# Retention with two mixture-of-experts layers: where the low halves of the second weight are made in the first slots

## The chip, the cores and the metric

The kernel runs on one core of a Trainium2 chip. The core has five engines with instruction queues of their own: TensorE (matrix products, called PE in the profile), VectorE (DVE), ScalarE (ACT), GpSimd (POOL) and SyncE (SP, which here issues transfers). The metric is the device time of one execution in microseconds (us), taken as the median over runs.

## The reference

The reference computes retention over 4 batches of 768 positions with 8 heads of 64 features, which gives 3072 tokens of 512 features, and passes these through two mixture-of-experts layers. Each layer sends every token to one of 8 experts, and an expert is two products with a ReLU in between. The second layer has one more gate on the output. Cut to what matters:

```python
def _moe_ref(x, modality_id, w_gate, modality_bias, w1, w2):
    logits = x @ w_gate + modality_bias[modality_id]
    e_idx = np.argmax(logits, axis=1)
    ...  # gate_w: softmax weight of the chosen expert
    for e in range(E):
        mask = e_idx == e
        h = np.maximum(x[mask] @ w1[e], 0.0)
        out[mask] = gate_w[mask, None] * (h @ w2[e])
    return out

def reference(**kwargs):
    attn_out = _attn_ref(**attn_kwargs)
    x = attn_out.transpose(0, 2, 1, 3).reshape(B * S, H * D)
    x = _moe_ref(x=x, **moe_kwargs)
    return _moe2_ref(x=x, **moe2_kwargs)
```

## The kernel before, in words

All products of the experts are done in pieces. A float32 operand is split into a high half (a copy rounded to the type fp32r, made by ScalarE) and a low half (what the rounding left, made by a subtraction), and one product becomes three: high by high, high by low, low by high. So each weight tile that is loaded (`raw1`, `raw2`) is turned into `w1h`, `w1l` and `w2h`, `w2l`. `split2` does this for the second weight: for each of four blocks of features it has ScalarE write `w2h` (L510) and an engine out of the list `los` write `w2l` (L511). A block of the second weight is a tile of 128 partitions by 1024 elements.

After retention, tokens are written to places in DRAM sorted by expert (`x1d` for the first layer, `x2d` for the second) with scatters that GpSimd issues (L469). A layer then runs over *slots* of 256 such rows, at least 12 and at most 19. A slot works like this:

- The rows are fetched (`fetch_rows`, L528 and L533), turned (L540) and split into `xh` and `xl` (L545, L547).
- The first product `mm1` (L891) runs over eight groups of 128 hidden features, 12 matmuls each, into four accumulators `hT`; after every second group `relu` has ScalarE write the high half `hh` (L882) and VectorE the low half `hl` (L883) of one of four blocks of hidden features.
- The second product `mm2` (L909) runs in eight steps of six matmuls: four steps for the first 128 rows, then four for the others. Step j uses blocks j of `hh`, `hl`, `w2h` and `w2l`; the second matmul of a step is the first that reads `w2l`.
- VectorE weighs the result (L915 or L917) and it is scattered, into `x2d` or into the output.

The routing of the tokens that a slot of layer 1 has made goes on inside the next slot, and the routing of the last tokens of the stage before goes on inside a layer's first slot. It is a chain of some 60 small VectorE steps. Logits go over `misc` (L588, or L945 to L954 in layer 2), the choice ends in `r_oh` (L207, L210), TensorE ranks the tokens (L215, L217), and from L221 on VectorE turns ranks into places, then into the table `r_meta` of the slots (to L359 the row positions, to L412 the experts). The two scatters of the last tokens follow the places, and the fetch of the next slot's rows follows these scatters.

Order is written out by hand: each engine runs its queue in the order of the code, and waits on semaphores for what the other engines produce. In `Slot.run`, `at(f)` runs the routing steps that are due at group f, then come `mm1(f)`, after odd f the `relu`, and in a layer's first slot (`first` is true) the splits of the second weight that are due at f. Later slots split the second weight only when the expert changes, in one piece and all on VectorE. The lines that the change and the prediction's steps touch are L1019 (the table of splits), L510 and L511, L882 and L883, the routing lines from L183 to L412, L469, L528, and the two products.

Of the kernel before, what the change touches and what calls it, by code (L numbers as in the profile page):

```python
# [416 lines left out]
def retention_moe_moe_kernel(ctx: ExitStack, tc: tile.TileContext, q, k, v, mod, mb, wg, wg2, w1, w2, cst_d, out):  # L417
    nc = tc.nc
# [89 lines left out]
    def split2(los=(nc.vector, nc.vector, nc.vector, nc.vector), ks=range(KF // 2)):  # L508
        for i in ks:
            nc.scalar.activation(w2h[i], raw2[i], AF.Copy)  # L510
            los[i].tensor_tensor(w2l[i], raw2[i], w2h[i], op=ALU.subtract)  # L511
# [91 lines left out]
    with ExitStack() as actx:  # L603
# [126 lines left out]
        for i in range(n):  # L730
# [37 lines left out]
            if i == 0:  # L768
# [3 lines left out]
                tr(1, "qT", "sq", halves=True)  # L772
                scale(2)
            run(*[f() for f in late.get(i, [])])
            for t in written.get(i, []):
                scatter1(t)
# [12 lines left out]
    with ExitStack() as mctx:  # L789
# [28 lines left out]
        class Slot:  # L818
# [153 lines left out]
            def steps(self, steps):  # L972
                by = {}
                for j, fs in list(steps):
                    by.setdefault(j, []).extend(fs)

                def at(j):
                    for f in by.get(j, []):
                        r = f()
                        if hasattr(r, "__next__"):  # L980
                            run(r)
                return at
# [22 lines left out]
            def run(self, steps=(), nxt=()):  # L1005

                at, first = self.steps(steps), self.first
                self.ids()
                if not first:
                    self.split2()  # L1010
                for f in range(KF):
                    at(f)
                    if f == 5:
                        self.prepare()
                    self.mm1(f)
                    if f % 2:
                        self.relu(f // 2)
                    if first:
                        split2([nc.gpsimd] * 2 + [nc.vector] * 2, ({0: (2, 0, 1), 1: (3,)}, {1: (2, 0), 2: (1, 3)})[self.li - 1].get(f, ()))  # L1019
                for j in range(8):  # L1020
                    at(8 + j)
                    if first and j == 5:
                        self.regs()
                        self.load(raw1, w1)
                        self.load(raw2, w2)
                    if j == (6 if first else 0):
                        self.split1(0)
                    if j == (7 if first else 2):
                        self.coming(nxt, Slot.xpose)
                        self.coming(nxt, Slot.xsplit)  # L1030
                        self.split1(1)
                    self.mm2(j // 4, range(2 * (j % 4), 2 * (j % 4) + 2))
                    if j % 4 == 3:
                        self.done(j // 4)
                at(16)
# [88 lines left out]
        def first2(pend):  # L1124
            g, steps = pend.route(FIRST_AT, banks=hT[2:])
            run(rp2.order())
            first(2, steps[:5], g, FIRST_AT[4], pend.scatter)
# [79 lines left out]
```

## Time and profile before

| | |
|---|---|
| median of three runs | 854.3 us (853.04 to 856.71) |
| the profiled execution | 853.39 us, of which the span from first to last instruction is 851.5 us |
| TensorE busy (matmuls) | 799.0 us, 94% of the span, mean granted clock 0.983 |
| VectorE busy | 430.3 us, 51% |
| ScalarE busy | 276.2 us, 32% |
| GpSimd busy | 202.1 us, 24% |

The first slot of layer 1 lies from about 153 to 184 us of the span, that of layer 2 from about 500 to 530 us. In a timeline row the first number is the start in us from the span's start, the second the duration in us, then come engine, line, operation, what is written and read with its shape, and how many instructions the row merges; in square brackets stands how long the engine was idle before, and what released it. In a row of stretches, the granted clock is a share of TensorE's full 2.4 GHz.

### The profile page before, as it was taken

The page shows a single profiled execution, that of the slowest core. Times are in us where ns is not written, and L with a number is a line of the kernel's source. Part 1 is how long each engine was busy: PE and PEld are TensorE (multiplying, and loading weights), DVE is VectorE, ACT ScalarE, POOL GpSimd, SP SyncE. Part 2 cuts the span into 40 slices and gives each one's busy share as a digit, 9 for nine tenths or more (in the row PEclk, how much of TensorE's full clock was granted, in tenths as well). Part 3 has the DMA queues.
Part 4 walks back from the last instruction along what each step waited for, and adds up shares of the span by engine and source line. Part 5 has one row for each costly group of instructions (what it writes and reads, how often), then busy time and mean ns, then how long its engine had stood idle before and what let it go on. Part 6 is the DMA issues. An engine that isn't in the chain of part 4 may idle for free. (4 is left out here: it accounts for less than half of the span.)

```text
span 851.5 us, 18413 instructions
## 1 busy us (share of the span) xinstructions
PE 799.0 (94%) x5987; PEld 696.2 (82%) x5987; DVE 430.3 (51%) x1110; ACT 276.2 (32%) x476; POOL 202.1 (24%) x291
## 2 busy tenths in 40 slices
PE   8999998799999998999999787999999999999992
PEld 7888877788889977888899576997889888888871
DVE  4554556744444338334454676144555673545921
ACT  3444445312122124121222451113252551514610
POOL 3455456712221011222210032011211112020210
PEclk9999999899999999999999999999999999999997
DMA  9987799272111015311222523412726385252610
GB/s 163 236 224 185 177 240 305 99 253 72 40 40 51 15 53 162 116 53 51 58 71 52 177 76 121 157 40 54 251 65 209 100 285 172 94 173 70 207 40 16
DMA packets 149688, 106.98 MB, mean 126 GB/s; under 512 B 94845, under 2 KB 125693, under 8 KB 149504
## 3 DMA queue, kind: packets, MB, share of 16 engines
q1 hardware_dynamic: 141664, 85.37, 37.2%
q0 software_dynamic: 6400, 18.98, 6.0%
q8 instruction: 73, 1.20, 0.6%
q14 instruction: 111, 0.91, 0.4%
q10 hardware_dynamic: 1440, 0.53, 0.3%
HBM read 167.64 MB, written 25.83 MB: 227 GB/s over the span
## 5 line engine op out<-in xcount | busy, mean ns | idle before, releaser
L891 PE MATMUL hT<-xh,w1h 128*128 128x256 f32 x768 | 222.4, 290 | 4.7 <-issue 2.9
L891 PE MATMUL hT<-xl,w1h 128*128 128x256 f32 x768 | 216.7, 282 | 1.4 <-DVE xl L547 1.4
L891 PE MATMUL hT<-xh,w1l 128*128 128x256 f32 x768 | 216.5, 282 | 0.0
L909 PE MATMUL po<-w2h,hh 128*128 128x512 f32 x432 | 172.6, 400 | 0.3
L909 PE MATMUL po<-w2l,hh 128*128 128x512 f32 x432 | 171.2, 396 | 0.0
L891 PEld LDWEIGHTS hT<-xh,w1h 128*128 128x128 f32 x768 | 146.4, 191 | 12.4 <-issue 11.0
L891 PEld LDWEIGHTS hT<-xl,w1h 128*128 128x128 f32 x768 | 146.6, 191 | 2.9 <-DVE xl L547 2.2
L891 PEld LDWEIGHTS hT<-xh,w1l 128*128 128x128 f32 x768 | 146.4, 191 | 0.0
L909 PE MATMUL po<-w2h,hl 128*128 128x512 f32 x432 | 136.3, 396 | 0.5 <-DVE hl L904 0.5
L883 DVE SCALAR_TENSOR_TENSOR hl<-hT,hh 128x512 fp32r<-128x512 f32 x96 | 65.5, 689 | 136.3 <-ACT hh L882 105.8
L882 ACT ACTIVATE hh<-hT 128x512 fp32r<-128x512 f32 x96 | 57.0, 596 | 201.7 <-PE hT L891 191.9
L909 PEld LDWEIGHTS po<-w2h,hl 128*128 128x128 f32 x432 | 81.1, 188 | 21.8 <-DVE hl L904 2.0
L909 PEld LDWEIGHTS po<-w2h,hh 128*128 128x128 f32 x432 | 81.6, 189 | 19.6 <-ACT hh L903 1.6
L909 PEld LDWEIGHTS po<-w2l,hh 128*128 128x128 f32 x432 | 81.6, 189 | 18.0
L469 POOL DMA_INDIRECT x2d<-ob,r_idx x28 | 29.6, 1059 | 261.0 <-DVE ob L260 174.5
L919 POOL DMA_INDIRECT out_dram<-ob,to x28 | 30.2, 1079 | 217.4 <-DVE ob L917 139.8
L545 ACT ACTIVATE xh<-xTb 128x512 fp32r<-128x512 f32 x58 | 33.5, 624 | 88.5 <-DVE xTb L540 79.7
L511 DVE TENSOR_TENSOR w2l<-raw,w2h 128x1024 fp32r<-128x1024 f32 x40 | 47.3, 1234 | 13.7 <-DMA xqb<-x1d 6.2
L506 DVE TENSOR_TENSOR w1l<-raw,w1h 128x512 fp32r<-128x512 f32 x80 | 49.8, 683 | 2.5 <-ACT w1h L505 2.5
L547 DVE TENSOR_TENSOR xl<-xTb,xh 128x512 fp32r<-128x512 f32 x58 | 37.6, 690 | 22.3 <-ACT xh L545 22.3
L505 ACT ACTIVATE w1h<-raw 128x512 fp32r<-128x512 f32 (+1 forms) x84 | 47.7, 640 | 0.0
L915 DVE TENSOR_SCALAR ob<-po,xmb 128x512 f32<-128x512 f32 x24 | 18.0, 750 | 54.5 <-PE po L909 54.5
(205 smaller groups left out, 997.9 us busy)
## 6 DMA issues: line engine op xcount, KB each, us to landing
raw<-in_w_dram SPq DMA_DIRECT2D x248, 512.0 KB
xqb<-x2d SPq DMA_DIRECT2D x124, 64.0 KB
xqb<-x1d SPq DMA_DIRECT2D x108, 64.0 KB
nq<-in_q_dram SPq DMA_DIRECT2D x24, 256.0 KB
nk<-in_k_dram SPq DMA_DIRECT2D x24, 256.0 KB
nv<-in_v_dram SPq DMA_DIRECT2D x24, 256.0 KB
x1d<-zrow SPq DMA_DIRECT2D x4, 516.0 KB
x2d<-zrow SPq DMA_DIRECT2D x4, 516.0 KB
```

The lines of the kernel that those rows point to most:

```text
L469: return nc.gpsimd.indirect_dma_start(out=dst, out_offset=bass.IndirectOffsetOnAxis(ap=rp.idx[:, t:t + 1], axis=0), in_=row, in_offset=Non ...
L505: nc.scalar.activation(w1h[i][:, cols], raw1[i][:, cols], AF.Copy)
L506: los[i].tensor_tensor(w1l[i][:, cols], raw1[i][:, cols], w1h[i][:, cols], op=ALU.subtract)
L511: los[i].tensor_tensor(w2l[i], raw2[i], w2h[i], op=ALU.subtract)
L545: nc.scalar.activation(hi[:, k:k + 2, :], xT[:, k:k + 2, :], AF.Copy)
L547: nc.vector.tensor_tensor(lo[:, k:k + 2, :], xT[:, k:k + 2, :], hi[:, k:k + 2, :], op=ALU.subtract)
L882: nc.scalar.activation(hh[b], hT[b], AF.Relu)
L883: nc.vector.scalar_tensor_tensor(hl[b], in0=hT[b], scalar=0.0, in1=hh[b], op0=ALU.max, op1=ALU.subtract)
L891: nc.tensor.matmul(to, lhsT=a[k][:, fs], rhs=b[:, k, :], start=(k == 0 and m == 0), stop=(k == KD - 1 and m == 2))
L909: nc.tensor.matmul(po[h], lhsT=x[b][:, o:o + P], rhs=w[f // 2][:, f % 2, :], start=(f == 0 and i == 0), stop=(f == KF - 1 and x is hl))
L915: nc.vector.tensor_scalar(perm(o[:, :DM]), plain(po[h]), gate, None, op0=ALU.mult)
L919: nc.gpsimd.indirect_dma_start(out=out, out_offset=bass.IndirectOffsetOnAxis(ap=to[:, t:t + 1], axis=0), in_=o[:, :DM], in_offset=None, bo ...
```

## The change

In the first slot of each layer the four low halves of the second weight were divided: blocks 0 and 1 on GpSimd, blocks 2 and 3 on VectorE, and they were done early, after groups 0 and 1 in layer 1 and after groups 1 and 2 in layer 2. Now all four are on VectorE, in the order of the blocks: in layer 1 after groups 0, 3, 5 and 7, in layer 2 after groups 1, 2, 5 and 7. The high halves, made by ScalarE in the same loop, move along. The programs of TensorE and SyncE are the same.

```diff
                     if first:
-                        split2([nc.gpsimd] * 2 + [nc.vector] * 2, ({0: (2, 0, 1), 1: (3,)}, {1: (2, 0), 2: (1, 3)})[self.li - 1].get(f, ()))
+                        split2([nc.vector] * 4, ({0: (0,), 3: (1,), 5: (2,), 7: (3,)}, {1: (0,), 2: (1,), 5: (2,), 7: (3,)})[self.li - 1].get(f, ()))
```

GpSimd's queue in layer 1's first slot, as a difference (`w2l_104` and `w2l_105` are the low halves of blocks 0 and 1; layer 2 loses the same two rows):

```order
 L854 TENSOR_SCALAR valid<-xmf,cst 128x1
 L856 COPY ob_2157<-xmf 128x2
-L511 TENSOR_TENSOR w2l_104<-raw_88,w2h_100 128x1024
-L511 TENSOR_TENSOR w2l_105<-raw_89,w2h_101 128x1024
 L469 DMA x1d<-yn_127,r_idx 26624x516 x2
 L810 TENSOR_LOAD r_meta
```

The scatters L469 now follow the small steps directly.

VectorE's queue in layer 1's first slot, from the first low half to the first step after the rank product. `hl_2147` and `hl_2148` are the low halves of hidden blocks 0 and 1. Before:

```order
L511 TENSOR_TENSOR w2l_106<-raw_90,w2h_102 128x1024
L583 COPY yl_125<-xT 128x128
L883 SCALAR_TENSOR_TENSOR hl_2147<-hT_116,hh_2143 128x512
L511 TENSOR_TENSOR w2l_107<-raw_91,w2h_103 128x1024
L588 COPY r_lg<-misc 128x8
...
L190 TENSOR_TENSOR rdz_626<-r_lg,rmx_623 128x16
L201 SCALAR_TENSOR_TENSOR rq_634<-rdz_626,cst 128x16
L205 TENSOR_REDUCE rm_0_637<-rq_634 128x2
L207 TENSOR_TENSOR r_oh<-rq_634,rm_0_637 128x16
L883 SCALAR_TENSOR_TENSOR hl_2148<-hT_117,hh_2144 128x512
L221 TENSOR_TENSOR rR_691<-misc,r_base 128x24
```

And now:

```order
L511 TENSOR_TENSOR w2l_104<-raw_88,w2h_100 128x1024
L583 COPY yl_125<-xT 128x128
L883 SCALAR_TENSOR_TENSOR hl_2147<-hT_116,hh_2143 128x512
L588 COPY r_lg<-misc 128x8
...
L190 TENSOR_TENSOR rdz_626<-r_lg,rmx_623 128x16
L201 SCALAR_TENSOR_TENSOR rq_634<-rdz_626,cst 128x16
L205 TENSOR_REDUCE rm_0_637<-rq_634 128x2
L207 TENSOR_TENSOR r_oh<-rq_634,rm_0_637 128x16
L883 SCALAR_TENSOR_TENSOR hl_2148<-hT_117,hh_2144 128x512
L511 TENSOR_TENSOR w2l_105<-raw_89,w2h_101 128x1024
L221 TENSOR_TENSOR rR_691<-misc,r_base 128x24
```

The second low half on this engine moved from ahead of the logits (L588) to behind `hl` of block 1, just ahead of L221. In the same way the one of block 2 (`w2l_106`) now stands behind `hl` of block 2 inside the chain of the places, between L345 and L347. The last one stands at the end of the routing. VectorE there, before:

```order
L409 CAST snx_2374<-r_meta 128x1
L411 SCALAR_TENSOR_TENSOR r_more<-r_last,snx_2374 128x1
L412 CAST r_sel<-r_more 128x1
L883 SCALAR_TENSOR_TENSOR hl_2150<-hT_119,hh_2146 128x512
L915 TENSOR_SCALAR ob_2157<-po_120,xmf 128x4x4x32
```

And now:

```order
L411 SCALAR_TENSOR_TENSOR r_more<-r_last,snx_2372 128x1
L412 CAST r_sel<-r_more 128x1
L883 SCALAR_TENSOR_TENSOR hl_2150<-hT_119,hh_2146 128x512
L511 TENSOR_TENSOR w2l_107<-raw_91,w2h_103 128x1024
L915 TENSOR_SCALAR ob_2157<-po_120,xmf 128x4x4x32
```

The low half of block 3 has become the last thing on VectorE before the result is weighed. In layer 2 the low halves of blocks 0 and 1 keep the two places that those of blocks 2 and 3 had (behind `hl` of block 0, and behind the copy L947), the one of block 2 stands behind `hl` of block 2 and ahead of L221, and the one of block 3 behind `hl` of block 3, between L359 and L369.

## Rows read from the trace of the kernel before

**Rows 1.** TensorE's waits: line, releaser: us in total, times, longest us

```profile
PE misc L215 <- DVE r_oh L207: 6.0, 2, 4.0
PE misc L952 <- DVE lT L947: 1.9, 1, 1.9
```

**Rows 2.** Timeline of layer 1's first slot: TensorE, GpSimd and VectorE

```profile
158.44 0.37 PE L891 MATMUL hT<-xh,w1h 128*128 128x256 f32 x1
...
161.50 4.67 POOL L511 TENSOR_TENSOR w2l<-raw,w2h 128x1024 fp32r<-128x1024 f32 x2
...
161.63 4.57 DVE L190 TENSOR_TENSOR rdz<-r_lg,rmx 128x16 f32<-128x16 f32 x1
...
166.87 0.17 PE L215 MATMUL misc<-r_oh,cb 128*128 128x16 bf16 x1 [3.98 <-DVE r_oh L207]
...
167.57 0.17 DVE L221 TENSOR_TENSOR rR<-misc,r_base 128x24 f32<-128x24 f32 x1
...
170.38 0.69 DVE L883 SCALAR_TENSOR_TENSOR hl<-hT,hh 128x512 fp32r<-128x512 f32 x1 [0.47 <-ACT hh L882]
...
172.81 0.39 PE L909 MATMUL po<-w2h,hh 128*128 128x512 f32 x1
...
174.24 0.68 DVE L883 SCALAR_TENSOR_TENSOR hl<-hT,hh 128x512 fp32r<-128x512 f32 x1
...
184.01 0.28 PE L891 MATMUL hT<-xh,w1h 128*128 128x256 f32 x1
```

**Rows 3.** Stretches: us; busy PE, PEld, DVE, ACT, POOL; clock; DMA share; GB/s

```profile
150.00:151.00 1.00, 1.00 (x8) 0.92 (x6) 0.97 (x5) 0.71 (x2) 0.75 (x1) 0.52 0.76 279
167.00:173.00 6.00, 6.00 (x40) 6.00 (x38) 5.32 (x42) 0.60 (x1) 2.06 (x2) 0.72 0.23 88
486.00:487.00 1.00, 0.97 (x6) 0.93 (x7) 1.00 (x1) 0.00 (x0) 0.00 (x0) 1.00 0.86 223
```

**Rows 4.** Timeline of layer 1's first slot: two ScalarE steps, hh and w2h

```profile
158.25 0.59 ACT L882 ACTIVATE hh<-hT 128x512 fp32r<-128x512 f32 x1
...
158.73 1.06 ACT L510 ACTIVATE w2h<-raw 128x1024 fp32r<-128x1024 f32 x1
```

**Rows 5.** Timeline of layer 2's first slot: VectorE and TensorE

```profile
507.18 0.42 DVE L947 COPY lT<-misc 128x256 f32<-128x256 f32 x1
...
511.14 0.18 DVE L954 COPY r_lg<-misc 128x32 f32<-128x32 f32 x1
...
511.56 1.32 DVE L190 TENSOR_TENSOR rdz<-r_lg,rmx 128x16 f32<-128x16 f32 x1
...
513.83 0.17 PE L215 MATMUL misc<-r_oh,cb 128*128 128x16 bf16 x1 [2.63 <-DVE r_oh L210]
...
514.35 0.17 DVE L221 TENSOR_TENSOR rR<-misc,r_base 128x24 f32<-128x24 f32 x1
...
517.80 0.15 DVE L359 TENSOR_SCALAR r_meta<-sd 128x1 int32<-128x1 f32 x1
...
518.03 0.63 PE L909 MATMUL po<-w2h,hh 128*128 128x512 f32 x1
```

**Rows 6.** Layer 2, slots 1 and 2 begin: timeline, and TensorE's branch (duration ns)

```profile
532.61 0.57 PE L891 MATMUL hT<-xh,w1h 128*128 128x256 f32 x1 [2.92 <-issue]
...
L1136 PEldq COMPARE_BRANCH  x1: 6109/6109/6109, 525.5 to 525.5; - x1
...
553.32 1.29 DVE L547 TENSOR_TENSOR xl<-xTb,xh 128x512 fp32r<-128x512 f32 x2 [0.76 <-ACT xh L545]
...
556.62 0.28 PE L891 MATMUL hT<-xh,w1h 128*128 128x256 f32 x1
```

**Rows 7.** Timeline: a low half and a scatter beside it; layer 2's second scatter

```profile
155.16 1.23 DVE L511 TENSOR_TENSOR w2l<-raw,w2h 128x1024 fp32r<-128x1024 f32 x1 [0.96 <-ACT w2h L510]
...
155.57 1.66 POOL L469 DMA_INDIRECT x1d<-yn,r_idx  x1 [0.30 <-issue]
...
517.97 0.97 POOL L469 DMA_INDIRECT x2d<-ob,r_idx  x1 [0.30 <-issue]
```

## The prediction, written before the change was run

> **What bounds the kernel now.** I read the page first: TensorE is busy 94% of the span and every other engine about half or less, so only what makes TensorE wait, or lowers its clock, can move the time. The list of TensorE's waits comes next [rows 1]. Its largest entries are waits of the rank product (L215) for `r_oh`, a small table that VectorE makes; one entry of 6.0 us for two waits has a longest of 4.0. That longest one stands in the stretch that the diff touches, layer 1's first slot, and the timeline shows why [rows 2]: VectorE's tiny L190 (16 elements a partition) runs 4.57 us, from 161.63 to 166.20, while GpSimd runs its two low halves of the second weight (L511) from 161.50 to 166.17. The two end together. L190 leads to `r_oh`, so TensorE waits 3.98 us before 166.87. The price does not end there. Over 167 to 173 the granted clock is 0.72 [rows 3], the lower of the two levels (1.2 GHz) for about half of the stretch. The same picture stands in layer 2's first slot [rows 5]: L190 takes 1.32 us where its neighbours take about 0.17, and the rank product waits 2.63 us.
>
> **Part by part, layer 1's first slot.** *Removed: GpSimd's two passes.* With them gone I let L190 take about 0.17. In the new order VectorE has no low half between `hl` of block 0 and the logits, so `r_oh` is made from about 159.5 on and is there near 161.2. TensorE would come to the rank product at 166.87 - 3.98 = 162.89. The wait goes whole: 3.98 us. The clock: from 158.44 to 162.89 TensorE ran 36 matmuls (three groups) in 4.45 us; from the rank product at 166.87 to the second product at 172.81 it ran 36 again and took 5.94 [rows 2]. So the slow stretch cost 1.49 us, and it goes with the wait. The second product starts at 172.81 - 5.47 = 167.3.
>
> *Added: two more low halves on VectorE, 1.23 us each [rows 7], in new places.* What is late next is the last one. Follow VectorE: block 1's sums are full after two of the three groups, at 158.44 + 24/36 x 4.45 = 161.4. ScalarE makes `hh` (0.59) and then the high half (1.06) [rows 4], which is ready at 163.1; the low half of block 1 ends at 164.4. Only then comes L221, the first step of the ranking. Before, L221 began at 167.57 and `hl` of block 3 at 174.24 [rows 2]; take off the 0.47 that VectorE waited in between (its row at 170.38) and the chain is 6.20 long. Now the low half of block 2 lies inside it: 164.4 + 6.2 + 1.2 = 171.8. Then `hl` (about 0.6) and the low half of block 3: 173.6, or 173.4 if neighbouring steps overlap as they do in the rows. TensorE's 48 matmuls of the second product took 184.01 - 172.81 = 11.2 us, 0.233 each. The second matmul of the fourth step, the twentieth, is the first that reads this last low half: 167.3 + 19 x 0.233 = 171.7. So a **new wait of 1.7 to 1.9 us** appears in the second product; I take 1.8. Does the clock fall after it? After a wait of 2.0 us (the other one of the pair in rows 1) it was 0.52 [rows 3]; after the 1.9 us for `lT` it stayed at 1.00 [rows 1, 3]. I take no fall, and keep 1.5 us as the other end. Net in layer 1: 5.5 - 1.8 = **3.7 us**, bounds 2.2 and 5.5. The hand-over to slot 1 showed no wait of TensorE (184.01 [rows 2]), and the rows it fetches go out earlier too.
>
> **Part by part, layer 2's first slot.** *Removed:* the wait of 2.63 us, and the slow clock behind it: 24 matmuls from 513.83 to 518.03 took 4.20, where 24/36 x 4.45 = 2.97 would do, so 1.23 us more. Does `r_oh` come in time? The copy of `lT` began at 507.18 and takes 0.42; low half 507.6 to 508.8; `hl` to 509.5. From L954 to the rank product was 513.83 - 511.14 = 2.69, of which 1.32 - 0.17 = 1.15 was the stall, so `r_oh` is ready near 511.0 [rows 5], and TensorE comes at 513.83 - 2.63 = 511.2. It fits by 0.2 us. The second product starts at 518.03 - 3.86 = 514.2.
>
> *Added:* block 2's sums are full at 511.2, so `hh`, high half and low half (0.1 + 0.6 + 1.06 + 1.23) end at 514.1 or 514.2, and L221 starts there, only about 0.2 us before its 514.35. So L359 ends near 517.7, `hl` at 518.4, the last low half at 519.6. TensorE wants it at 514.2 + 19 x 0.233 = 518.6: a new wait of 1.0 us. The product ends 3.86 - 1.0 = 2.9 us earlier, some 0.3 more if its first matmuls (0.63 at 518.03) are no longer slow: 3.1.
>
> *But that does not pass on whole.* The rows for the next slots are fetched after the ranking and the two scatters, and these hardly move. Slot 1 began at 532.61 after 2.92 us with no releaser that the profile names; TensorE's queue stood in a branch from 525.5 for 6.11 us [rows 6]. I let that branch begin 3 us earlier and be no later than the rest. Slot 2 then decides: its `xl` is made from 553.32 to 554.61, behind a fetch that queues behind eight weight loads, and TensorE came to it at 556.62 [rows 6]. That slack is 2.0 us. If the fetch keeps its time, TensorE can be at most 2.0 us early there; the remainder becomes a wait. I take **1.9 us** for layer 2, bounds 0.8 (below) and 3.1.
>
> **A move past GpSimd's queue.** Its scatters (L469), which stood behind its two passes, now stand beside VectorE's low halves of blocks 2 and 3. A scatter that began while a low half ran (155.16 to 156.39) took 1.66 us; layer 2's second one, with no low half beside it, took 0.97 at 517.97 [rows 7]. So up to 0.7 us per scatter, on the way to the fetch. In layer 1 the fetch has about 3 us of its own gain to pay with. In layer 2 it comes off the cap: 2.0 - 0.7 = 1.3, and no change of the fetch gives 2.0 or 2.2; I stay near the upper end since the scatter is half done before the low half starts. Of this the Trainium skill says, SBUF — State Buffer, section "SBUF: two separate sides", that the pair of ports which VectorE and GpSimd share is locked for a whole instruction, and that a GpSimd-issued DMA can starve since its descriptors cannot be written meanwhile. By that rule the scatter would lose the whole low half, 1.23 us, which speaks against the change; the row's 1.66 against 0.97 is half of that.
>
> **The sum.** 3.7 + 1.9 = 5.6 us off the profiled execution's 853.39 us gives 847.8. That execution lies 0.9 us below the median of the three runs (854.3), so I forecast **848.7**.
>
> **The rivals.** (1) *The clock falls at the new wait in layer 1.* The wait is 1.7 to 1.9 and the rows put the border between 1.9 and 2.0, so this is close. Price 1.5 us: gain 4.1, time 850.2. (2) *Everything passes.* VectorE's small steps pack tighter than I added them, the last low halves come before TensorE needs them, and the weight loads of layer 2 start earlier as well: 5.5 + 3.1 to 3.9, about 8.9, time 845.4. Against it: the chain of 6.2 us is measured work, and the fetch hangs on it. (3) *Layer 2's rows come late.* The second scatter loses the whole 1.2 us beside the last low half, and the cap shrinks to 0.8: gain 4.5, time 849.8. (4) *Slower.* The lock works both ways, and the two scatters hold the low halves of blocks 2 and 3 for their own length, up to 1.66 each, 3.3 a slot. Then TensorE waits 5.1 in layer 1 and 4.3 in layer 2, the clock falls in both (1.5, 1.2), and the sum is 5.5 - 6.6 + 3.9 - 5.5 = -2.7: 857.0. It decides from about 2.2 us of stretch a slot in layer 1 (5.5 - 1.8 - 1.5). Against it: the low half beside the scatter took its usual 1.23 [rows 7]. (5) *The stall of L190 has another cause* and stays; then nothing is gained and the time is 854. That both stalled steps end with GpSimd's pass speaks against it.
>
> **How the numbers follow.** Chances: forecast 0.50, (1) 0.20, (2) 0.13, (3) 0.12, (4) 0.03, (5) 0.02. The range holds the forecast with its bounds, (1) and (3), and stops short of (2) and (4): 845.8 to 851.6. About 0.5%, 4.3 us, is what a measurement of this kernel can tell from no change, so the border is at 850.0. Nearly all of the forecast, (2), more than half of (3) and somewhat under half of (1) lie below it: faster 0.70. (4) is itself only 0.3% slower; 0.03 stands for it and for what I have not seen. The rest, 0.27, is within.
>
> **What would show it.** In the changed kernel's profile GpSimd has no L511; L190 takes 0.2 us in both slots; the waits of 4.0 and 2.6 for `r_oh` are gone and the clock is full between rank product and second product. In their place TensorE's list has a wait of the second product (L909) for `w2l`, near 1.8 us in layer 1 and 1.0 in layer 2, and waits for `xl` at slots 1 and 2 of layer 2 that add up to what layer 2 does not pass on. The prediction is wrong if the `w2l` waits are absent or above 2 us with a slow clock behind, if L190 stays long, or if layer 2's slot 2 starts by the same amount earlier as its second product did.

## The result, and the profile after

The changed kernel took 845.45 us (median of four, 842.52 to 849.72) beside 854.96 us for the kernel before (median of four, 853.04 to 856.71): a ratio of 0.989, 95% interval 0.9858 to 0.9922. That is faster by over 0.5%, as forecast, and 0.35 us below the range of 845.8 to 851.6. The forecast itself was 848.7. Executions of one kernel differ here by 7 us and more, so four of them leave the size loose; two more comparisons follow below. The profiled execution of the changed kernel took 849.72 us, its slowest, with a span of 847.9 us; the one before took 853.39.

The page of the changed kernel (busy time, share of the span, instructions) says what was moved: four more instructions on VectorE, four fewer on GpSimd.

```profile
PE 800.3 (94%) x5987; PEld 695.4 (82%) x5987; DVE 430.0 (51%) x1114; ACT 276.7 (33%) x476; POOL 190.1 (22%) x287
```

TensorE's waits in the changed kernel (line, releaser: us in total, times, longest), against [rows 1]:

```profile
PE hT L891 <- ACT xh L545: 3.1, 1, 3.1
...
PE misc L952 <- DVE lT L947: 2.4, 1, 2.4
PE po L909 <- DVE w2l L511: 2.3, 2, 1.6
...
PE misc L215 <- DVE r_oh L207: 2.1, 1, 2.1
```

The pair of waits for `r_oh` of 6.0 us has become a single one of 2.1 (the one at 150 us, ahead of the slot that the diff touches). It shows the same picture as the one that went: GpSimd makes low halves there too, those of the first weight (L506), L190 ends with them, and the change leaves them where they were:

```profile
145.56 4.68 POOL L506 TENSOR_TENSOR w1l<-raw,w1h 128x1024 fp32r<-128x1024 f32 x2 [3.32 <-ACT w1h L505]
148.21 2.06 DVE L190 TENSOR_TENSOR rdz<-r_lg,rmx 128x16 f32<-128x16 f32 x1
```

New are two waits of the second product for `w2l`, and one at the start of a slot for `xh`. The timeline of layer 1's first slot, against [rows 2] (start, duration, engine, line; in brackets the idle time before and its releaser):

```profile
160.67 0.28 PE L587 MATMUL misc<-cst,yl 128*128 128x8 f32 x2
...
162.83 0.17 DVE L190 TENSOR_TENSOR rdz<-r_lg,rmx 128x16 f32<-128x16 f32 x1
...
165.10 0.18 PE L215 MATMUL misc<-r_oh,cb 128*128 128x16 bf16 x1
...
166.62 0.18 DVE L221 TENSOR_TENSOR rR<-misc,r_base 128x24 f32<-128x24 f32 x1
...
169.46 1.22 DVE L511 TENSOR_TENSOR w2l<-raw,w2h 128x1024 fp32r<-128x1024 f32 x1
...
169.51 0.39 PE L909 MATMUL po<-w2h,hh 128*128 128x512 f32 x1
...
170.32 1.20 POOL L469 DMA_INDIRECT x1d<-yn,r_idx  x1 [0.30 <-ACT hh L882]
...
174.45 1.22 DVE L511 TENSOR_TENSOR w2l<-raw,w2h 128x1024 fp32r<-128x1024 f32 x1
...
175.72 0.49 PE L909 MATMUL po<-w2l,hh 128*128 128x512 f32 x1 [1.62 <-DVE w2l L511]
...
182.59 0.28 PE L891 MATMUL hT<-xh,w1h 128*128 128x256 f32 x1
```

L190 takes 0.17 instead of 4.57, the rank product has no wait, and the second product waits 1.62 us for the last low half. The stretches of the changed kernel (busy PE, PEld, DVE, ACT, POOL; granted clock; DMA share; GB/s), against [rows 3], have the clock at its higher level (2.4 GHz) from 167 to 182, so also behind that new wait:

```profile
167.00:173.00 6.00, 6.00 (x38) 5.32 (x37) 5.79 (x44) 2.97 (x4) 2.29 (x2) 1.00 0.24 89
173.00:176.00 3.00, 1.38 (x6) 0.85 (x5) 2.56 (x9) 0.00 (x0) 0.00 (x0) 1.00 0.03 6
176.00:182.00 6.00, 6.00 (x27) 4.82 (x27) 2.00 (x2) 0.48 (x1) 1.24 (x5) 1.00 0.76 190
```

Layer 2 of the changed kernel, against [rows 5, 6]:

```profile
510.99 0.17 DVE L190 TENSOR_TENSOR rdz<-r_lg,rmx 128x16 f32<-128x16 f32 x1
...
512.35 0.18 PE L215 MATMUL misc<-r_oh,cb 128*128 128x16 bf16 x1
...
514.12 1.23 DVE L511 TENSOR_TENSOR w2l<-raw,w2h 128x1024 fp32r<-128x1024 f32 x1 [0.25 <-ACT w2h L510]
...
515.27 0.17 DVE L221 TENSOR_TENSOR rR<-misc,r_base 128x24 f32<-128x24 f32 x1
...
518.88 0.97 POOL L469 DMA_INDIRECT x2d<-ob,r_idx  x1 [0.30 <-issue]
...
520.66 0.51 PE L909 MATMUL po<-w2l,hh 128*128 128x512 f32 x1 [0.72 <-DVE w2l L511]
...
530.82 0.39 PE L891 MATMUL hT<-xh,w1h 128*128 128x256 f32 x1 [3.12 <-ACT xh L545]
...
552.73 1.25 DVE L540 STREAM_TRANSPOSE xTb<-xqb 128x1024 f32<-128x1024 f32 x1 [7.02 <-DMA xmb<-x2d]
...
555.32 0.28 PE L891 MATMUL hT<-xh,w1h 128*128 128x256 f32 x1
```

The stall of L190 and the wait for `r_oh` are gone here too, `w2l` is waited for 0.72 us, and slot 1 waits 3.12 us for `xh`, that is for its rows. Before, that start had shown 2.92 us with no releaser. From the layer's first group, at 500.12 (500.38 before), slot 1 starts after 30.7 us (32.2 before), slot 2 after 55.2 (56.2).

One difference lies far from both slots, at the very end. From the end of the last matmul to the end of the span it is 16.7 us before and 14.5 now, and the difference stands in GpSimd's queue: between the last scatter and the last instructions of that queue (L1164, behind the last slot). The last matmul and these instructions (times, number, shortest, median and longest in ns, first and last start in us), before:

```profile
834.16 0.63 PE L909 MATMUL po<-w2h,hl 128*128 128x512 f32 x2
L1164 POOLq EVENT_SEMAPHORE  x5: 17/17/43, 841.6 to 842.0; - x5
```

and now:

```profile
832.77 0.63 PE L909 MATMUL po<-w2h,hl 128*128 128x512 f32 x2
L1164 POOLq EVENT_SEMAPHORE  x5: 17/17/43, 837.7 to 838.0; - x5
```

### The profile page after: what moved, and what is told of

It is laid out like the page before. It is cut to its first block, busy times and chain, and to the rows that moved or that the text cites. A ratio compares the mean times of both kernels' runs of the same rounds, so it can differ in the third digit from the quotient of the medians.

```text
span 847.9 us, 18399 instructions
## 1 busy us (share of the span) xinstructions
PE 800.3 (94%) x5987; PEld 695.4 (82%) x5987; DVE 430.0 (51%) x1114; ACT 276.7 (33%) x476; POOL 190.1 (22%) x287
## 5 line engine op out<-in xcount | busy, mean ns | idle before, releaser
L891 PEld LDWEIGHTS hT<-xh,w1h 128*128 128x128 f32 x768 | 145.9, 190 | 13.4 <-issue 8.0
L883 DVE SCALAR_TENSOR_TENSOR hl<-hT,hh 128x512 fp32r<-128x512 f32 x96 | 65.4, 689 | 134.6 <-ACT hh L882 103.5
L469 POOL DMA_INDIRECT x2d<-ob,r_idx x28 | 29.6, 1056 | 277.1 <-DVE ob L260 155.6
L511 DVE TENSOR_TENSOR w2l<-raw,w2h 128x1024 fp32r<-128x1024 f32 x44 | 51.6, 1220 | 13.1 <-DMA xqb<-x1d 6.9
L506 DVE TENSOR_TENSOR w1l<-raw,w1h 128x512 fp32r<-128x512 f32 x80 | 49.8, 683 | 2.5 <-ACT w1h L505 2.5
L540 DVE STREAM_TRANSPOSE xTb<-xqb 128x1024 f32<-128x1024 f32 x29 | 36.0, 1242 | 24.3 <-DMA xmb<-x2d 13.9
```

The source lines that it names most:

```text
L469: return nc.gpsimd.indirect_dma_start(out=dst, out_offset=bass.IndirectOffsetOnAxis(ap=rp.idx[:, t:t + 1], axis=0), in_=row, in_offset=Non ...
L506: los[i].tensor_tensor(w1l[i][:, cols], raw1[i][:, cols], w1h[i][:, cols], op=ALU.subtract)
L540: nc.vector.transpose(xT.rearrange("p k (a i) -> p a k i", i=32), xq.rearrange("p a (k i) -> p a k i", k=KD))
L883: nc.vector.scalar_tensor_tensor(hl[b], in0=hT[b], scalar=0.0, in1=hh[b], op0=ALU.max, op1=ALU.subtract)
L891: nc.tensor.matmul(to, lhsT=a[k][:, fs], rhs=b[:, k, :], start=(k == 0 and m == 0), stop=(k == KD - 1 and m == 2))
```

## The experiments

Times are against runs of the kernel before on the same chip. The gains in us are worked out from the ratios and 853.6 us, the mean of the 89 executions of the kernel before in these comparisons (847.59 to 859.09). In the excerpts of edits a line is cut to the part that differs; its lines with a minus are the changed kernel's where nothing else is said.

| | kernel | median us | ratio (95%) | gain us |
|---|---|---|---|---|
| a1 | changed, second comparison | 845.36 | 0.9923 (0.9895 to 0.9951) | 6.6 |
| a2 | layer 1 alone | 848.42 | 0.9944 (0.9916 to 0.9973) | 4.8 |
| a3 | layer 2 alone | 850.54 | 0.9969 (0.9944 to 0.9993) | 2.6 |
| a4 | low halves one place earlier | 846.4 | 0.9919 (0.9889 to 0.9949) | 6.9 |
| b1 | before, again | 852.64 | 0.9990 (0.9964 to 1.0016) | 0.9 |
| b2 | VectorE, old places | 845.64 | 0.9898 (0.9864 to 0.9932) | 8.7 |
| b3 | GpSimd, new places | 851.97 | 0.9975 (0.9955 to 0.9995) | 2.1 |
| c1 | changed, layer 2 chain first | 844.88 | 0.9892 (0.9866 to 0.9918) | 9.2 |
| d1 | layer 1 of b2, layer 2 of c1 | 842.79 | 0.9873 (0.9854 to 0.9892) | 10.8 |
| d2 | changed, third comparison | 843.91 | 0.9889 (0.9870 to 0.9909) | 9.5 |
| d3 | layer 2 of c1 alone | 849.54 | 0.9943 (0.9918 to 0.9968) | 4.9 |
| e1 | one GpSimd pass left | 848.92 | 0.9947 (0.9929 to 0.9966) | 4.5 |

**How large, and in which layer.** The first four runs set the forecast's sum, layer by layer (theory S), against a reading in which everything passes (theory P). The first is the changed kernel itself; the next two keep one layer's first slot as it was.

> The changed kernel once more, unaltered, in five rounds. Theory S (the forecast's steps and sizes hold, and the four executions of the first comparison fell apart by chance): 5.6 us faster than the kernel before, ratio about 0.9934. Theory P (more passes through than the steps allow, because layer 2 is not held by its row fetch, or because the new waits cost nothing): 9.5 us faster, ratio about 0.989. In this trace, with S: a wait of TensorE for the last low half of 1.5 to 1.9 us in layer 1 and 0.7 to 1.0 us in layer 2, and the fetch of layer 2's slots 1 and 2 ends TensorE's waits there.

Layer 1 alone:

```diff
-split2([nc.vector] * 4, ({0: (0,), 3: (1,), 5: (2,), 7: (3,)}, {1: (0,), 2: (1,), 5: (2,), 7: (3,)}) ...
+split2(([nc.vector] * 4 if self.li == 1 else [nc.gpsimd] * 2 + [nc.vector] * 2), ({0: (0,), 3: (1,), 5: (2,), 7: (3,)}, {1: (2, 0), 2: (1, 3)}) ...
```

> Only layer 1's first slot is changed; layer 2's first slot has the old table and GpSimd. Theory S: 3.7 us faster than the kernel before (bounds 2.2 and 5.5). Theory P: 5.5 us faster. In the trace the wait for the ranking table in layer 2's first slot (2.6 us) is still there, the one of 4.0 us in layer 1 is gone.

Layer 2 alone:

```diff
-split2([nc.vector] * 4, ({0: (0,), 3: (1,), 5: (2,), 7: (3,)}, {1: (0,), 2: (1,), 5: (2,), 7: (3,)}) ...
+split2(([nc.vector] * 4 if self.li == 2 else [nc.gpsimd] * 2 + [nc.vector] * 2), ({0: (2, 0, 1), 1: (3,)}, {1: (0,), 2: (1,), 5: (2,), 7: (3,)}) ...
```

> Only layer 2's first slot is changed; layer 1's first slot has the old table and GpSimd. Theory S: 1.9 us faster than the kernel before (bounds 0.8 and 3.1). Theory P: 3.9 us faster. In the trace the wait of 4.0 us in layer 1 is still there.

The changed kernel gained 6.6 us (4.2 to 9.0), layer 1 alone 4.8 and layer 2 alone 2.6: the layers add up within their intervals (2.3 to 7.2 and 0.6 to 4.8), and layer 1 brings nearly two thirds, as forecast (3.7 of 5.6). For the whole, the sum's 5.6 lies inside the interval, and theory P's 9.5 just outside. The first comparison had given 9.5, so more executions had to tell the size.

The last of the four takes the new wait away by making each low half one place earlier.

```diff
-({0: (0,), 3: (1,), 5: (2,), 7: (3,)}, {1: (0,), 2: (1,), 5: (2,), 7: (3,)})
+({0: (0, 1), 3: (2,), 5: (3,)}, {0: (0,), 1: (1,), 2: (2,), 5: (3,)})
```

> As the changed kernel, but every low half one place earlier, so that the last one no longer stands behind the last hidden block: layer 1 after groups 0, 0, 3 and 5, layer 2 after groups 0, 1, 2 and 5. Theory S: the wait for the last low half (1.6 us in layer 1, 0.7 in layer 2) goes; layer 1 gives 5.3 instead of 3.7, layer 2 stays at its 1.9 because the row fetch decides there, so 7.2 us faster than the kernel before and 1.6 faster than the changed kernel. Theory P: no difference to the changed kernel beyond 0.5 us, since the new waits cost nothing.

In its trace the second product of layer 1 has no wait and takes 11.33 us instead of 13.08. So the wait is what was costed, and it is VectorE's last low half. The time, 6.9 us less, doesn't tell it from the 6.6 beside it: a difference of 1.75 us in one slot is below what these runs resolve.

**The engine or the places?** Two kernels do one half of the change each. In what was expected of them, theory E is that the engine matters, and theory S now stands for the spread places. All on VectorE, at the old places:

```diff
-({0: (0,), 3: (1,), 5: (2,), 7: (3,)}, {1: (0,), 2: (1,), 5: (2,), 7: (3,)})
+({0: (2, 0, 1), 1: (3,)}, {1: (2, 0), 2: (1, 3)})
```

> All four low halves on VectorE, but at the old places (early, ahead of the logits). Theory E (what costs is GpSimd's pass, which holds VectorE's small step L190; the places matter little): L190 takes 0.17 us in both first slots, in layer 1 VectorE had 2.4 us of idle time between 156.4 and 158.9 that takes the two more passes, so no wait for r_oh and none for w2l, L587 to rank product near 4.4 us and the second product 11.2; in layer 2 two more passes ahead of the logits make r_oh some 1 us late, the wait for w2l (0.72) goes. Time 6 to 7.5 us less than the kernel before, ratio near 0.992. Theory S (the spread places are what helps; four passes ahead of the logits only put VectorE's own 2 x 1.23 us where GpSimd's pass was): wait for r_oh 2.5 to 3.0 us in each layer, time 0 to 2 us less, ratio 0.998 to 1.000.

At the new places, with blocks 0 and 1 on GpSimd:

```diff
-split2([nc.vector] * 4, ...
+split2([nc.gpsimd] * 2 + [nc.vector] * 2, ...
```

> GpSimd keeps the low halves of blocks 0 and 1, but all four stand at the new places. Theory E with its mechanism (a small VectorE step with two operands from SBUF stands until the GpSimd pass beside it ends, 2.3 us each): in layer 1 GpSimd's first pass begins behind its own small steps near 161.7 and holds L190 about 1.2 us, which costs TensorE under 1 us; its second pass lies beside L221, which then stands up to 2.3 us, and the chain with the last low half comes about 1 us later, so that the wait of the second product for w2l grows from 1.6 to some 2.7; in layer 2 L190 stands about 1 us. Time 1 to 4.5 us less than before, about 3.5, ratio near 0.996. Theory S (places alone): like the changed kernel, 6.6 us less, ratio 0.992, and L190 short. A theory in which GpSimd's passes hold VectorE wherever they stand, by their whole 4.7 us: 0, ratio 1.000.

The engine alone gained 8.7 us, the places alone 2.1. Theory E held for both; its 6 to 7.5 us for the first and 1 to 4.5 for the second lie inside the intervals (5.8 to 11.6 and 0.4 to 3.8). In the engine-only kernel VectorE does three low halves in what had been idle time, and the rank product has no wait:

```profile
155.81 3.50 DVE L511 TENSOR_TENSOR w2l<-raw,w2h 128x1024 fp32r<-128x1024 f32 x3 [0.96 <-ACT w2h L510]
...
164.40 0.17 PE L215 MATMUL misc<-r_oh,cb 128*128 128x16 bf16 x1
```

In the places-only kernel no L190 of layer 1 is held: GpSimd's first pass meets a step ahead of it, L183, which takes 1.18 us, and the second pass meets another VectorE step, in the chain behind the rank product (timeline of layer 1's first slot, and two stretches of it):

```profile
163.94 2.41 POOL L511 TENSOR_TENSOR w2l<-raw,w2h 128x1024 fp32r<-128x1024 f32 x1 [2.21 <-ACT w2h L510]
164.01 2.37 DVE L318 TENSOR_TENSOR sni<-r_base,cst 128x8 int32<-128x8 f32 x1
...
168.62 1.22 DVE L511 TENSOR_TENSOR w2l<-raw,w2h 128x1024 fp32r<-128x1024 f32 x1
168.96 1.71 POOL L469 DMA_INDIRECT x1d<-yn,r_idx  x1 [0.30 <-issue]
...
174.86 0.80 PE L909 MATMUL po<-w2l,hh 128*128 128x512 f32 x1 [2.60 <-DVE w2l L511]
```

```profile
171.00:176.00 5.00, 2.40 (x9) 1.64 (x8) 3.67 (x21) 0.00 (x0) 0.00 (x0) 0.83 0.36 99
176.00:183.00 7.00, 7.00 (x28) 5.60 (x27) 3.29 (x4) 1.15 (x2) 1.25 (x5) 0.87 0.76 229
```

L318, eight elements a partition, takes 2.37 us and ends with GpSimd's pass. The chain is late by it, and the wait for `w2l` is 2.60, near the 2.7 that was written down. Behind it the clock is below full, and the second product takes 15.36 us: 11.2 of work, 2.6 of waiting and 1.56 of slow clock. That is the prediction's first rival with its price of 1.5 us, on the other side of the border: after 1.62 us of waiting in the same place the clock stayed at 1.00.

A third run halves the suspected cost, with one GpSimd pass instead of two. Its edit against the kernel before:

```diff
-split2([nc.gpsimd] * 2 + [nc.vector] * 2, ...
+split2([nc.gpsimd] + [nc.vector] * 3, ...
```

> The kernel before with one change: GpSimd makes only the low half of block 0 in the first slots, that of block 1 goes to VectorE at its old early place. Theory E (a VectorE step with two operands from SBUF stands until the GpSimd pass beside it ends, so the stall is as long as the passes that are left): one GpSimd pass of 2.3 to 2.4 us in layer 1, the VectorE step beside it ends with it, TensorE waits 1.0 to 2.0 us for r_oh instead of 3.8 to 4.0; in layer 2 the one pass is over before the logits come, no stall, and r_oh is late by VectorE's own work alone, by under 1 us. From L587 to slot 1 in layer 1: 22.4 to 24 us, against 25.5 to 26.4 before and 21.9 in the changed kernel. Time 5.5 to 8 us less than before, ratio 0.991 to 0.9935. Theory H (the handing over between the two engines costs a fixed time, however much GpSimd does): stall still 4 us and more, wait for r_oh 3.8 to 4.0, time 0 to 2 us less.

Layer 1 of this kernel:

```profile
162.71 2.48 DVE L201 SCALAR_TENSOR_TENSOR rq<-rdz,cst 128x16 f32<-128x16 f32 x1
162.78 2.37 POOL L511 TENSOR_TENSOR w2l<-raw,w2h 128x1024 fp32r<-128x1024 f32 x1
...
165.65 0.17 PE L215 MATMUL misc<-r_oh,cb 128*128 128x16 bf16 x1 [1.09 <-DVE r_oh L207]
```

and layer 2:

```profile
504.57 2.49 POOL L511 TENSOR_TENSOR w2l<-raw,w2h 128x1024 fp32r<-128x1024 f32 x1 [9.24 <-ACT w2h L510]
...
505.47 3.81 DVE L511 TENSOR_TENSOR w2l<-raw,w2h 128x1024 fp32r<-128x1024 f32 x2 [0.34 <-ACT w2h L510]
...
511.35 0.17 PE L215 MATMUL misc<-r_oh,cb 128*128 128x16 bf16 x1 [2.58 <-DVE r_oh L210]
```

In layer 1 the stall is one pass long, so the length of GpSimd's work sets it and not the handing over; this time L201 was the step beside it. From L587 to slot 1 it is 21.5 us, even less than the 22.4 to 24 expected, and 4.3 less than before. In layer 2 the expectation was wrong. I had GpSimd's pass end ahead of the logits, which it does (507.06), but I had overlooked that VectorE's own low half, which came at 505.47, stands beside it as well: the pair takes 3.81 us instead of about 2.35, the logits are late by that and by the extra pass, and TensorE waits 2.58 us for `r_oh`, as before. The gain of 4.5 us (2.9 to 6.1), less than the 5.5 to 8 expected in the middle, is about what layer 1's slot gave.

**What layer 2 hands back.** In layer 2 the low half of block 2 stands ahead of L221, and the scatters, the fetch of slot 1's rows, the loads of the raw weights and the fetch of slot 2's rows follow L221. One edit puts both last low halves behind the chain; c1 has it with layer 1 changed, d3 with layer 1 as before. The table of layer 2:

```diff
-{1: (0,), 2: (1,), 5: (2,), 7: (3,)}
+{1: (0,), 2: (1,), 7: (2, 3)}
```

> The changed kernel, but in layer 2 the low half of block 2 stands behind the chain of the places too, just ahead of that of block 3. L221 begins near 1.2 to 1.4 us earlier against the rank product, and so do the two scatters; TensorE then waits 0.8 to 1.0 us for w2l of block 2 in the second product. Theory F (what takes back layer 2's gain at slots 1 and 2 is the fetch of the rows, which hangs on the scatters): from the rank product, the raw-weight loads and the rows for slots 1 to 3 come 1.2 us earlier and the stretch from layer 2's first group to slot 3 is 0.8 to 1.4 us shorter than in the changed kernel, 1 us less in time, ratio 0.991. Theory Q (it is TensorE's own branch with its instruction loads, or the weights): no change of the stretch beyond 0.3 us, ratio 0.992 as the changed kernel's.

> Layer 1 as before, with GpSimd; only layer 2 changed, with the low halves of blocks 2 and 3 behind the chain. Theory F (what layer 2 does not pass on is the rows of slot 2, which hang on L221 through the scatters, the fetch and the weight loads): L221 stands near 13.4 us behind the layer's first group (13.9 to 14.4 before, up to 15.1 in the changed kernel), L540 of slot 2 near 50.8, and the time is 3.0 to 4.5 us less, 0.995 to 0.9965, against 2.6 with the changed kernel's own table for layer 2. Theory Q (slots 2 and 3 are held by something that does not move): 2.6 or less, 0.997.

From the traces, in us behind layer 2's first group:

| layer 2's order, traces of | slot 2's L540 | slot 1 | slot 2 | slot 3 |
|---|---|---|---|---|
| before: before, b1, a2 | 50.9, 50.8, 50.7 | 32.2, 32.4, 31.7 | 56.2, 57.7, 55.0 | 92.5, 92.7, 91.1 |
| changed: after, a1, a3, d2 | 52.6, 52.8, 54.6, 49.8 | 30.7, 28.2, 29.8, 28.3 | 55.2, 54.9, 56.6, 53.0 | 91.0, 92.8, 94.0, 88.4 |
| chain first: c1, d1, d3 | 50.8, 50.3, 49.7 | 27.6, 27.5, 26.6 | 52.8, 52.3, 51.7 | 90.9, 88.9, 88.3 |

The mean gain of the changed order is 2.9 us at slot 1, 1.4 at slot 2 and 0.6 at slot 3; with the chain first 4.9, 4.1 and 2.7. So the rows take gain back, as theory F has it: in twelve of the fourteen traces SyncE issues the fetch of slot 1's rows 6.14 to 6.17 us after L221, whatever the order (6.4 in e1 and 7.7 in a4, for a reason that stays open). With the chain first L221 stands 12.4 to 13.4 us behind the first group, with the changed order 13.7 to 15.2, and slots 1 and 2 begin earlier in each of the three traces than in any of the four. By slot 3 the means differ by 2 us, but one trace with the changed order (d2) has slot 3 at 88.4 as well, so this size isn't resolved, and c1's 90.9 misses the 0.8 to 1.4 us that theory F wrote for it. The price in the second product is a wait for `w2l` of 0.65 us in c1, no more than the changed kernel's 0.72, and in d3 the chain came even earlier than expected (L221 at 12.4 us, not 13.4). In time the chain-first layer 2 alone gained 4.9 us (2.7 to 7.0), against 2.6 (0.6 to 4.8) with the changed order, and c1's 9.2 lies between the changed kernel's three results. The intervals overlap; the direction agrees with the traces and isn't shown by the times alone. What is handed back behind slot 2 is, where it is seen, a wait for rows and the slow clock after it. At slot 2 of the second trace of the changed kernel (a1):

```profile
550.29 1.25 DVE L540 STREAM_TRANSPOSE xTb<-xqb 128x1024 f32<-128x1024 f32 x1 [9.61 <-DMA xmb<-x2d]
...
552.31 0.39 PE L891 MATMUL hT<-xh,w1h 128*128 128x256 f32 x1 [1.86 <-ACT xh L545]
```

```profile
552.00:557.00 5.00, 4.35 (x24) 4.15 (x25) 2.70 (x4) 0.77 (x2) 1.09 (x1) 0.72 0.02 6
```

The kernel before had no wait at that place [rows 6].

**The two together, the third comparison, and the yardstick.** The last version has the layer 1 of b2 and the layer 2 of c1:

```diff
-({0: (0,), 3: (1,), 5: (2,), 7: (3,)}, {1: (0,), 2: (1,), 5: (2,), 7: (3,)})
+({0: (2, 0, 1), 1: (3,)}, {1: (0,), 2: (1,), 7: (2, 3)})
```

> All low halves on VectorE; layer 1 at the old early places, layer 2 with those of blocks 2 and 3 both behind the chain of the places. Theory C (the layers add up, and what is saved ahead of the second product counts): layer 1's first slot 26.0 us from its first group to slot 1, with no wait for r_oh or w2l, 1.5 us less than in the changed kernel; layer 2 as with the chain first, slot 2 some 53 us behind the layer's first group. Time 8.5 to 10 us less than the kernel before, ratio 0.988 to 0.990. Theory R (the rows of layer 2's slots 2 and 3 hand everything beyond some 7 us back): 6.5 to 7.5 us less, 0.991 to 0.992.

> The changed kernel again, beside the other two on one chip. Theory C: 7 us less than the kernel before, ratio 0.992, which lies between the 9.5 us of the first comparison and the 6.6 us of the second. If the forecast's 5.6 were the true size: 0.9934; if the first comparison's: 0.989. In the trace, layer 1's stretch from L587 to slot 1 is 21.9 us (25.8 before), and the rows of layer 2's slot 2 are turned (L540) 52.5 us or more behind the layer's first group, where the kernel before has 50.8.

> The kernel before once more, as a yardstick: all theories expect a ratio of 1.000 with an interval that holds it, and a second trace in which L190 takes 4.5 us in layer 1 and 1.3 in layer 2, the waits for r_oh are 3.9 to 4.0 and 2.6, and the second product of layer 1's first slot starts 5.9 to 6.5 us after the rank product. How far its other stretches differ from the first trace says what chance does: retention up to the first slot, the end of layer 1, and the first three slots of layer 2 by 1 us or more each.

The kernel with both orders took 842.79 us and gained 10.8 (9.2 to 12.5): theory C, slightly more than expected, and a version that beats the kernel before by more than the changed one did in any comparison. Beside the changed kernel of the same call (843.91) it is 1.1 us less, which isn't resolved. Its stretch from L587 to slot 1 in layer 1 is 20.17 us, against 21.92 in the changed kernel.

The changed kernel in its third comparison gained 9.5 us, outside what theory C wrote for it (7, ratio 0.992, where the interval is 0.9870 to 0.9909), and its rows for layer 2's slot 2 came at 49.8 us, where 52.5 or more was written down. Over all 18 executions, taken together although they come from several chips, its mean is 845.7 us (842.52 to 849.72), that of 89 executions of the kernel before 853.6: 7.8 us with a 95% interval of about 6.7 to 9.0.

The kernel before, run as if it were a change, came out at 0.999. In its second trace it wasn't L190 that stood beside GpSimd's passes but the low half just ahead of it:

```profile
160.21 4.71 POOL L511 TENSOR_TENSOR w2l<-raw,w2h 128x1024 fp32r<-128x1024 f32 x2
160.91 5.09 DVE L511 TENSOR_TENSOR w2l<-raw,w2h 128x1024 fp32r<-128x1024 f32 x1 [0.26 <-ACT w2h L510]
```

Here L190 took 0.17, not the 4.5 that was written down, and the wait for `r_oh` was 3.78 all the same. Whichever step with two operands in SBUF comes is held; the steps with one, such as the copies and `hl`, ran through.

## Why the prediction was right, and where it was not

**The cause and the new waits: right.** L190's stall was GpSimd's passes: without them it is gone wherever the low halves stand, with one pass it is one pass long, and at other places another step is held. With them gone, the rank product comes 4.1 us earlier behind L587 (8.36 to 8.70 us in four traces with the old layer 1, 4.43 to 4.53 in five with the new one; forecast 3.98). From the rank product to the second product it is 4.4 us instead of 5.9 to 6.5 (forecast: 1.49 less). The second product takes 13.08 instead of 11.2, 1.88 more (forecast 1.8). From L587 to slot 1 this makes 25.8 (from the row below to 184.01 in [rows 2]) against 21.9 us: 3.9 where 3.7 was forecast.

```profile
158.19 0.39 PE L587 MATMUL misc<-cst,yl 128*128 128x8 f32 x2 [0.72 <-DVE yl L583]
```

The first rival, a fall of the clock at this wait, didn't happen at 1.62 us and did at 2.60. That it didn't is partly luck, for the border between 1.9 and 2.0 us that the prediction read from two rows doesn't hold: at the start of layer 2's slot 2 a wait of 1.75 us left the clock full in d1 (first row), and one of 1.71 us at the same place in c1 (second row) didn't.

```profile
549.00:554.00 5.00, 4.24 (x33) 4.05 (x34) 2.85 (x5) 1.48 (x3) 1.09 (x1) 1.00 0.02 5
549.00:554.00 5.00, 4.42 (x22) 4.23 (x23) 2.70 (x4) 0.70 (x2) 1.08 (x1) 0.66 0.03 6
```

**The scatters.** The prediction took from [rows 7] that a scatter beside a low half loses up to 0.7 us. In layer 1's first slot of the changed kernel one of the two scatters came during a low half, and it lost 0.23 us (1.20 instead of 0.97). The rows show by what: the scatter that ran 170.32 to 171.52 ends 0.84 us after the low half that ended at 170.68; the one of the places-only kernel, 168.96 to 170.67, ends 0.83 after its low half (169.84); that of [rows 7], 155.57 to 157.23, 0.84 after (156.39). So the end of such a scatter follows the end of the low half, and it loses most of what was left of that when it came; the "half of that" in the prediction was only the point at which the scatter came. The Trainium skill (SBUF — State Buffer, section "SBUF: two separate sides") has the shared ports locked for the whole instruction, and the stalls here agree. But the starved DMAs that the prediction took from that section are told there of VectorE's two-port modes, which the section denies to a `tensor_tensor` such as the low half, and its probe saw none beside one; the scatters here were delayed beside one all the same, and the measurement decides. They read their places `r_idx` from SBUF; whether that is the reason no run here shows. In layer 2 the second scatter came 0.51 us ahead of the low half (519.39) and took its 0.97, so the charge against layer 2 did not fall due, and the third rival's neither.

**Layer 2: the step that failed.** The forecast took 2.0 us of slack at slot 2, from the end of `xl` to TensorE's first matmul, and passed 1.9 on. But the first matmul waits for `xh` alone: in the waiting traces it follows L540's start by 2.02 us. The kernel before had 5.30 there (from the row below to the matmul at 556.62 in [rows 6]), so the slack was 3.3, and 2.3 and 4.8 in two other traces of that order.

```profile
551.32 1.25 DVE L540 STREAM_TRANSPOSE xTb<-xqb 128x1024 f32<-128x1024 f32 x1 [4.32 <-DMA xmb<-x2d]
```

The other half of the step failed too: the fetch did not keep its time. In three of four traces slot 2's rows came 1.8 to 3.7 us later, in one 1.1 earlier; part of that is L221, which stands 13.7 to 15.2 us behind the layer's first group instead of 14.0 to 14.4. The remainder lies between the first fetch and the second, 22.8 to 25.7 us in the four traces with the changed order and 23.4 to 24.0 in the three with the old, and what varies it stays open. So in place of the 1.9 us that the forecast passed on, the traces show 0.6 by slot 3.

**The end of the kernel: a term put at nothing.** The forecast let slot 2 decide and carried its gain to the end of the kernel unchanged. From slot 3 to the last matmul that holds: 241.9 us on average in the three traces of the old order, 241.8 in the four of the changed one. But from the end of the last matmul to the end of the span it is 16.4 to 16.7 us in all five traces in which GpSimd makes low halves in layer 2's first slot (before, a2, b1, b3, e1) and 14.4 to 14.5 in the nine others; GpSimd's low halves in layer 1 make no difference to it (a3 and d3 have them). That is 2.2 us more that the change gives, and no step of the prediction has it. Most of it stands between GpSimd's last scatter and its next instructions: 3.1 us before (838.5 to 841.6), 1.0 now (836.7 to 837.7). Why the end of that queue depends on what GpSimd did in layer 2's first slot, over 300 us earlier, stays open. With it the traces agree with the timed runs: layer 2 alone 0.6 + 2.2 = 2.8 against 2.6 (0.6 to 4.8), the chain-first layer 2 alone 2.7 + 2.2 = 4.9 against 4.9.

**Why the time left the range.** The base was 854.3, the median of three; the mean of 89 executions is 853.6, which is 0.7 us of it. The gain is 7.8 instead of 5.6: the traces have 3.9 in layer 1's slot (0.2 more than forecast), 0.6 in layer 2 by slot 3 (1.3 less) and 2.2 at the end (not forecast), 6.7 together, and 1.1 us can't be placed, which is inside the interval (6.7 to 9.0). The median of the first four executions lay 0.3 below the mean of all 18. The range reached only to a gain of 8.5, because the second rival (all passes, 845.4) was left outside at 0.13. That its time is the result to a tenth of a microsecond is luck, since its mechanism isn't what happened: both waits for `w2l` are there, and in the traces layer 2 has handed back half of its gain by slot 2.

**The cheaper change.** The prediction costed both halves of the edit together. By the timed runs nearly all of the gain is the engine (8.7 us at the old places): VectorE had the room there, and the spreading is what put the last low half in the way of the second product.

## What to carry to other kernels

When a tiny step on VectorE takes microseconds, look at which GpSimd instruction ends with it; moving that instruction elsewhere in time moved the stall to another step here and gained little (b3), and moving the work to VectorE costs its own short time, in idle time if there is some. Before counting a gain, find where the next rows or weights are hung up (here the chain of small steps, the scatters, the fetch), measure the slack to the first operand that is really waited for, and reckon with the clock charging a second time behind a new wait. Compare the two traces to their last instruction, also where the edit touches nothing. And take a base and a result from many executions where they scatter by more than the effect: one profiled execution may lie 4 us off its kernel's mean.

## What the runs showed of the hardware

- Held by GpSimd's passes were VectorE steps of several kinds, all with both operands in SBUF: L511 5.09 us instead of 1.23, L318 2.37, and L201, a SCALAR_TENSOR_TENSOR, 2.48 instead of 0.18. `hl` (L883), which reads `hT` from PSUM and `hh`, took its 0.68 or 0.69 everywhere, also beside a pass.
- The hold goes both ways. In layer 2 of the kernel before, GpSimd's second pass came while a low half of VectorE ran (508.88 to 510.62), and the two passes took 5.80 us, where those of layer 1 took 4.67 [rows 2]:

```profile
507.04 5.80 POOL L511 TENSOR_TENSOR w2l<-raw,w2h 128x1024 fp32r<-128x1024 f32 x2 [9.07 <-ACT w2h L510]
...
508.88 1.74 DVE L511 TENSOR_TENSOR w2l<-raw,w2h 128x1024 fp32r<-128x1024 f32 x1 [1.28 <-ACT w2h L510]
```

- A low half takes 2.4 us on GpSimd and 1.2 on VectorE, so the change made the work itself shorter besides.
- The length of a wait alone doesn't tell whether the clock falls: 1.62 us ahead of a matmul within the second product left it at 1.00 in all five traces that have it (the changed kernel's three, a2 and c1); at the start of layer 2's slot 2, 1.86 us in a1 was followed by 0.72 and 1.71 in c1 by 0.66, while 1.75 in d1 left it at 1.00.
- The end of a kernel can depend on work long before it: 14.4 to 14.5 or 16.4 to 16.7 us from the last matmul to the end of the span, by whether GpSimd had low halves in layer 2's first slot. The reason isn't shown.
